# New places in the instruction order around the second and third routing of an attention and mixture-of-experts kernel

## The chip, the cores and the metric

The kernel runs on one core of one Trainium2 chip. The metric is the device time of one execution in microseconds. Three runs of the kernel before took 711.42, 707.03 and 711.97 us; their median is 711.42 us.

## The reference

First comes an attention over q, k, v of shape (8, 8, 576, 64). It is the sum of two: a full attention over sequences averaged in groups of four, its output repeated four times, and a local one, in which a position sees those less than four away. Its output, seen as 4608 tokens of 512 numbers, is the input of a layer with 8 experts. A gate gives each token a logit for each expert. All logits are gone through from the largest down, and a token goes to the expert of the logit if the token is still free and the expert has fewer than 576 tokens:

```
for idx in np.argsort(-flat):
    tok, e = idx // E, idx % E
    if assigned[tok] >= 0 or counts[e] >= cap: continue
    assigned[tok] = e; counts[e] += 1
out[mask] = np.maximum(x[mask] @ w1[e], 0) @ w2[e]     # mask: tokens of e
```

w1[e] is 512 by 1024, w2[e] is 1024 by 512.

## The kernel before

**Stages.** Attention takes the first 276 us. Then each expert has a routing, which finds the next expert that fills up and the list of its 576 tokens, a gather of these tokens, a split of its weights and an MLP. The routing for the next expert runs beside the MLP of the present one, so that eight MLPs stand one behind the other. Below, "the first MLP" is that of the first expert, and "the third routing" is the one that makes the third expert's list; it runs beside the second MLP, and it begins at the end of the first.

**Routing** (`phase`, L1007). A threshold is found in six rounds: three on the high 16 bits of the keys, three on the low ones. A round (`count`, L856) compares all keys with 64 or 32 thresholds (VectorE, L822; the first of each half is `first_compare`, L836, into a tile `level`), counts with 18 or 9 small matmuls (L871), takes differences and a flag (L881, L884), adds the flags up in one matmul (L889) and makes the next thresholds (L894 to L901). Between the halves stands a sum of the tokens above the threshold (`totals`, L917), behind the sixth round two matmuls that rank the chosen tokens (L928, L929), eighteen that make the list (L1131), and another sum. These matmuls make 17 groups, whose first ones are kept in `self.groups`. The list itself, `idx`, is four VectorE instructions (L1144); the last is `done`.

**Gather** (L1208). Five indirect DMAs of GpSimd (L1217) fetch 128, 128, 128, 128 and 64 tokens. For the first two experts TensorE turns each piece with four transposes (L1234), whose result ScalarE copies to fp16 (L1238) and whose rest VectorE makes (L1239, kept in `self.lows`: places 0 to 4 belong to the first expert, 5 to 9 to the second). Later experts turn their pieces by DMA (L1248). Pieces 0 and 1, and 2 and 3, share a PSUM tile of two banks.

**Weights** (`split`, L1190). Eight slices: ScalarE makes the fp16 high part (L1200), VectorE two halves of the low part (L1202). Slices 0 to 3 belong to w1, and are asked for behind the output of chunks 0 to 3 of the MLP in front.

**MLP** (L1262). Eight times twelve matmuls with 256 columns (pieces 0 and 1) and as many with 320 (pieces 2 to 4) make the hidden layer (L1279). Then five chunks of 24 matmuls with 512 columns (L1320) make the output; `second[c, j]` is matmul j of chunk c. A list `marks` has each matmul's place in the order, counted in microseconds of columns at 2.4 GHz; one MLP is 46.08 long on that scale.

**Order.** Each engine takes its instructions in a fixed order. A planner makes it from priorities and its own estimate of times; `behind_` (L832) and `issue_after` put an instruction behind another of its engine without a wait in the hardware. What matters here:

- `SPIN` (L1352): filler matmuls in front of the first MLP (L1186): 44, then the transposes of piece 0, 6 more, piece 1, 4 more, the MLP.
- `BEHIND` (L1344): the second routing's ranking behind `second[1, 6]`, its list behind `second[2, 2]` of the first MLP.
- `GET0` (L1343): the second expert's pieces 0 and 1 are asked for behind chunk 3 of the first MLP, 2 to 4 behind chunk 4.
- `PACE` and `PACES` (L1350): from the third routing on, a place for each of the 17 groups. A place less 19 is a mark in the MLP beside that routing; a negative one counts back from 47 in the MLP in front (`place`, L1253). A group isn't put in front of its place; how far behind it comes is the planner's choice. The third routing uses `PACE`, the fourth a table of its own.

Of the kernel before, what the change touches and what calls it, by code (L numbers as in the profile page):

```python
# [12 lines left out]
OP = mybir.AluOpType  # L13
# [722 lines left out]
LOP = 512  # L736
# [27 lines left out]
class Routing:  # L764
# [71 lines left out]
    def first_compare(self, i, key):  # L836
        cmp = self.compare(self.level[i], key, self.first, 0, NT)
        for ins in self.listed:
            self.behind_(cmp, ins)
        return self.level[i]  # L840

    def busy(self, n, mm):

# [163 lines left out]
    def phase(self, last, first=False, known=None):  # L1007

        nc, wk = self.nc, self.wk
        B3 = [128, E, NT]  # L1010

        def t(name, dt=BF, shape=(128, NT)):
            return wk.tile(list(shape), dt, name=name)
# [15 lines left out]
        if first:  # L1029
            self.pads = self.ps.tile([128, 2, 512], F32, name="pH", bufs=2)[:, 0, :E * NT]  # L1030
            xh = self.v["xh"]
            early = self.level[0]
# [5 lines left out]
        kh, kl = [self.v["s"].bitcast(I16)[:, o::2] for o in (1, 0)]  # L1038

        if not first:  # L1040
            early = self.first_compare(0, xh)
        if first:
            cmp0 = self.level[1]
            H = self.count(oh, xh, early, lambda: self.cap, None, lambda: self.compare(cmp0, xl, self.first, self.rest, NT))
        else:
            H = self.count(oh, xh, early, lambda: self.cap)
            cmp0 = self.first_compare(1, xl)
        e = t("e")
        nc.vector.tensor_scalar(e, kh, H, None, op0=OP.is_equal)
        ol = t("ol", BF, (128, E, NT))  # L1050
# [98 lines left out]
class Experts:  # L1149
# [40 lines left out]
    def split(self, raw, first):  # L1190

        nc = self.nc
        w = {}

        def piece(k):
            r = raw[k // 2][:, 1024 * (k % 2):1024 * (k % 2) + 1024]
            hi = self.wt.tile([128, 1024], F16, name=f"wh{k}")
            lo = self.wt.tile([128, 1024], F16, name=f"wl{k}")
            sc = W1S if k < 4 else W2S
            nc.scalar.activation(hi, r, AF.Copy, scale=sc)  # L1200
            for a in range(0, 1024, LOP):
                nc.vector.scalar_tensor_tensor(lo[:, a:a + LOP], r[:, a:a + LOP], sc, hi[:, a:a + LOP],  # L1202
                                               op0=OP.mult, op1=OP.subtract)
            w[k] = (hi, lo)

        return w, piece
# [133 lines left out]
TOP = 10 ** 6  # L1340
WS = {0: (4,), 1: (5,), 2: (6,), 3: (7,)}
GET = {0: (0, 1), 1: (2, 3), 2: (4,)}
GET0 = {3: (0, 1), 4: (2, 3, 4)}  # L1343
BEHIND = ((1, 6), (2, 2))  # L1344
TURN = (6, 12, 18)
NXT = 1
SPAN = 47.0
LAST = (2, 2.7, 10.4)
LEAD = -19.0
PACE = (0.6, 4, 10.5, 13, 15.3, 17, 18.5, 19.2, 21.5, 24, 26.5, 30, 32.5, 36.5, 37.2, 43.9, 43)  # L1350
PACES = {2: (0.6, 4, 10.5, 13.9, 16.2, 18, 19.5, 20.4, 22.5, 24.8, 27, 30, 32.5, 36.5, 37.2, 43.9, 43)}
SPIN = (44, 6, 4)  # L1352


def moe_attention(tc, q, k, v, wg, w1, w2, cst, out):
    nc = tc.nc
    with ExitStack() as top:
# [13 lines left out]
        with ExitStack() as ctx:  # L1371
# [21 lines left out]
            for i in range(E):  # L1393
                mine = split
                more = i + 1 < E
                if more:
                    with tc.high_priority(), tc.issue_after(ex.lows[NXT].ins if i == 0 else ro.done.ins) if i < 2 else nullcontext():
                        idx2, raw = ro.phase(i + 2 == E, False, lambda ei: ex.weights(ei, False))
                    w2_, split = ex.split(raw, False)
                    xt2, piece2 = ex.gather(idx2, False, i + 1 < ROWS)  # L1400
                    if i < FREE:
                        for k in range(8):
                            split(k)

                def in1(f, ins):
                    if f in WS:
                        with tc.issue_after(ins.ins), tc.high_priority(TOP if i == 0 else None):
                            for k in WS[f]:
                                mine(k)

                def in2(c, ins, mm):
                    if i == 0:
                        with tc.issue_after(mm.ins):
                            for j in GET0.get(c, ()):
                                piece2(j)
                    if more:
                        with tc.issue_after(ins.ins):
                            for j in GET.get(c, ()) if i else ():
                                piece2(j)
                            if c < 4:  # L1420
                                with tc.issue_after(ro.done.ins) if c and i == 0 else nullcontext():
                                    split(c)

                ex.mlp(w, xt, idx, in1, in2, i == 0)
                if i == 0:
                    ro.behind_(ex.products[0], ex.spins[2][-1])
                    for at, mms in zip(TURN, ex.turns[2:5]):
                        for mm in mms:
                            ro.behind_(mm, ex.products[at])
                    for at, mms in zip(BEHIND, ro.late):  # L1430
                        for mm in mms:
                            ro.behind_(mm, ex.second[at])
                elif more:
                    ex.place(i, ro.groups)
                ro.behind = ex.turned if i == 0 else None
                if more:
                    idx, w, xt = idx2, w2_, xt2
# [54 lines left out]
```

## Time and profile before

| | us |
|---|---|
| runs of the kernel before | 711.42, 707.03, 711.97 |
| median | 711.42 |
| the profiled execution's own time | 709.79 |
| its span, first to last instruction | 708.1 |
| attention | 0 to 276.0 of the span |
| rest of the first routing, filler and first transposes | 276.0 to 290.3 |
| eight MLPs | 290.3 to 697.5 |

The span is 1.7 us shorter than the profiled execution's time, which is 1.6 us below the median. TensorE is busy for 403.06 of the 407.20 us of the MLPs, VectorE for 290.85, ScalarE for 154.76. The granted clock is 1.00 there and 0.72 on average in the 14.3 us in front of them. Times of rows below are microseconds from the start of the span.

### The profile page before, as it was taken

What the parts mean: (1) busy time and instruction counts of PE and PEld (TensorE: products, weight loads), DVE (VectorE), ACT (ScalarE), POOL (GpSimd) and SP (SyncE); (2) the same over time, 40 slices, a digit from 0 to 9 for tenths busy, and PEclk for the clock granted to TensorE, in tenths of its full rate; (3) what the DMA queues carried; (4) which work ended last, traced back from release to release, by engine and by line L of the source; (5) the groups of instructions that cost most, each with busy time, mean ns of one, the idle gap of its engine ahead of it and who ended that gap; (6) DMA issues with size and microseconds to landing.
All of it is one profiled execution on the core that took longest, in us unless ns stands there. A gap on an engine that the chain in (4) does not pass through costs nothing.

```text
span 708.1 us, 21934 instructions
## 1 busy us (share of the span) xinstructions
PE 649.8 (92%) x8938; PEld 451.0 (64%) x8938; DVE 533.6 (75%) x1562; ACT 337.7 (48%) x650; POOL 232.7 (33%) x303
## 2 busy tenths in 40 slices
PE   6888999889999845999999999999999999999994
PEld 4667878778787733774574575575674674755741
DVE  5798889987989977887889697797797876634500
ACT  4567778787785521532532443443444424424410
POOL 4865374644737420402402303204104106202011
PEclk9899999999999975999999999999999999999997
DMA  9967859777785632605507617638348269814001
GB/s 263 245 157 218 227 159 245 205 205 202 197 238 160 192 117 89 218 1 181 192 1 283 157 43 269 129 116 229 95 183 204 55 233 198 313 35 100 1 31 38
DMA packets 132157, 113.73 MB, mean 161 GB/s; under 512 B 81240, under 2 KB 109912, under 8 KB 132056
## 3 DMA queue, kind: packets, MB, share of 16 engines
q1 hardware_dynamic: 124760, 90.76, 45.0%
q0 software_dynamic: 6432, 20.98, 9.5%
q8 instruction: 71, 1.16, 0.7%
q10 hardware_dynamic: 864, 0.58, 0.3%
q14 instruction: 30, 0.25, 0.1%
HBM read 85.74 MB, written 19.46 MB: 149 GB/s over the span
## 4 chain that ended last, share of the span: by engine, by line
PE 45%; DVE 22%; issue 17%; ACT 5%; DMA 5%; POOL 4%; SPq 1%; ACTq 0%; POOLq 0%; DVEq 0%
PE pH L1279 13%; PE pX L1320 11%; PE g L574 3%; PE pR L871 2%; DVE wl L1202 2%; PE g L327 2%; POOL out_dram L1330 2%; DVE x L453 2%; PE g L552 2%; PE g L592 2%; PE s L532 1%; DVE qt L311 1%; POOL xg L1217 1%; PE g L407 1%; PE pH L1186 1%
## 5 line engine op out<-in xcount | busy, mean ns | idle before, releaser
L1279 PE MATMUL pH<-xt,wh 128*128 128x256 f16 (+1 forms) x1024 | 191.3, 286 | 1.2 <-ACT xt L1238 0.5
L1320 PE MATMUL pX<-wh,ht 128*128 128x512 f16 (+1 forms) x640 | 178.0, 379 | 0.0
L1279 PE MATMUL pH<-xt,wl 128*128 128x320 f16 (+1 forms) x512 | 144.6, 286 | 0.0
L1320 PEld LDWEIGHTS <-ht 128*128 128x128 f16 (+1 forms) x960 | 82.6, 100 | 93.9 <-issue 3.8
L1320 PE MATMUL pX<-wl,ht 128*128 128x512 f16 (+1 forms) x320 | 117.6, 379 | 0.0
L1279 PEld LDWEIGHTS <-wh 128*128 128x128 f16 x1024 | 97.5, 98 | 30.2 <-issue 5.7
L1330 POOL DMA_INDIRECT out_dram<-y,idx x40 | 43.0, 1074 | 177.8 <-ACT y L1327 153.5
L1303 ACT ACTIVATE ht<-pH 128x512 f16<-128x512 f32 (+1 forms) x128 | 45.5, 407 | 112.5 <-PE pH L1279 112.5
L1202 DVE SCALAR_TENSOR_TENSOR wl<-nat,wh 128x512 f16<-128x512 f32 x128 | 83.5, 687 | 14.9 <-ACT wh L1200 8.3
L1327 ACT ACTIVATE y<-pX 128x512 f32<-128x512 f32 (+1 forms) x40 | 23.8, 594 | 103.4 <-PE pX L1320 54.3
L1306 DVE SCALAR_TENSOR_TENSOR ht<-pH,ht 128x512 f16<-128x512 f32 (+1 forms) x128 | 52.3, 450 | 24.4 <-ACT ht L1303 23.9
L1200 ACT ACTIVATE wh<-nat 128x1024 f16<-128x1024 f32 x64 | 67.3, 1053 | 4.1 <-DMA nat<-in_moe_w_dram 4.1
L1217 POOL DMA_INDIRECT xg<-x_dram,idx x40 | 42.5, 1062 | 61.9 <-DVE used L1100 33.4
L1279 PEld LDWEIGHTS <-wl 128*128 128x128 f16 x512 | 49.9, 98 | 12.7 <-issue 0.8
L563 ACT COPY pt<-g 64x512 f32<-64x512 f32 x72 | 41.8, 581 | 28.8 <-PE g L552 27.8
L574 PE MATMUL g<-vw,pt 128*64 128x65 f32 x1152 | 45.5, 229 | 5.6 <-issue 2.7
L574 PEld LDWEIGHTS g<-vw,pt 128*64 128x64 f32 x1152 | 39.6, 142 | 12.7 <-issue 6.6
L327 PE MATMUL g<-ident,nat 128*128 128x128 f32 x256 | 40.4, 283 | 3.9 <-DMA nat<-in_q_dram 3.3
L313 ACT COPY kt<-g 64x512 f32<-64x512 f32 (+1 forms) x60 | 38.3, 639 | 6.2 <-PE g L327 5.2
L1246 DVE SCALAR_TENSOR_TENSOR xs<-xg,xs 128x512 f16<-128x512 f32 (+1 forms) x30 | 20.3, 688 | 26.8 <-ACT xs L1245 15.7
L1019 POOL MEMSET f<- 128x1 bf16 x8 | 0.8, 106 | 116.3 <-DVE sumf L925 44.2
L300 POOL TENSOR_TENSOR gtmp<-kt 128x576 f32<-128x576 f32 x14 | 16.1, 1147 | 61.4 <-ACT kt L313 43.6
(221 smaller groups left out, 1153.0 us busy)
## 6 DMA issues: line engine op xcount, KB each, us to landing
nat<-in_moe_w_dram SPq DMA_DIRECT2D x28, 1024.0 KB
vw<-in_v_dram SPq DMA_DIRECT2D x136, 78.0 KB
x_dram<-x SPq DMA_DIRECT2D x36, 256.0 KB
nat<-in_q_dram SPq DMA_DIRECT2D x32, 256.0 KB
nat<-in_k_dram SPq DMA_DIRECT2D x32, 256.0 KB
nat<-in_v_dram SPq DMA_DIRECT2D x28, 256.0 KB
up<-up_dram SPq DMA_DIRECT2D x9, 256.0 KB
nat<-in_moe_w_dram SPq DMA_DIRECT2D x4, 512.0 KB
```

Source lines behind the costliest of these rows:

```text
L313: self.nc.scalar.copy(out, in_)
L327: nc.tensor.transpose(p[:, a, :, fp], src[:, 4 * hh + 2 * a + s, 2 * fp:2 * fp + 2].rearrange("p f d -> p (f d)"), self.ident)
L563: self.nc.scalar.copy(out, in_)
L574: nc.tensor.matmul(o[64 * i:64 * i + 64, 65 * h:65 * h + 65], pt[:, 2 * (h % 2) + i, 2 * g + h // 2].rearrange("p b q -> p (b q)"), self.v ...
L1200: nc.scalar.activation(hi, r, AF.Copy, scale=sc)
L1202: nc.vector.scalar_tensor_tensor(lo[:, a:a + LOP], r[:, a:a + LOP], sc, hi[:, a:a + LOP], op0=OP.mult, op1=OP.subtract)
L1217: self.fetched = nc.gpsimd.indirect_dma_start(out=xg[:n], out_offset=None, in_=self.x, in_offset=bass.IndirectOffsetOnAxis(ap=idx[:n, c:c ...
L1279: mm = nc.tensor.matmul(p[:, s, :s1 - s0], w[d][a][:, 128 * f:128 * f + 128], xt[:, b, d, s0:s1], start=j == 0, stop=j == len(seq) - 1)
L1303: last = nc.scalar.activation(hi, q, AF.Relu)
L1306: low = nc.vector.scalar_tensor_tensor(lo, q, 0.0, hi, op0=OP.max, op1=OP.subtract)
L1320: mm = nc.tensor.matmul(p[o:o + m], ht[:, f, h0:h0 + m], w[4 + f // 2][b][:, 512 * (f % 2):512 * (f % 2) + 512], start=j < parts, stop=j > ...
L1330: i = nc.gpsimd.indirect_dma_start(out=self.out, in_=y[:n], in_offset=None, out_offset=bass.IndirectOffsetOnAxis(ap=idx[:n, c:c + 1], axis=0))
```

## The change

- The first run of filler matmuls in front of the first MLP goes from 44 to 36.
- The second expert's list goes from behind `second[2, 2]` to behind `second[2, 0]`. Its piece 0 is asked for behind chunk 2 instead of chunk 3 of the first MLP, and piece 2 behind chunk 3 instead of chunk 4. Each piece's transposes get a place: behind `second[3, 20]`, `[4, 2]`, `[4, 8]`, `[4, 14]` and `[4, 20]`. The last two are still asked for behind the end of chunk 4.
- On VectorE, the low parts of the second expert's slice 0 go behind the finished list, those of slice 2 behind the rest of piece 0, and those of slice 3 behind the rest of piece 1. The third routing's first comparison of low bits goes behind the rest of piece 0 as well.
- The third routing gets a table of places of its own, the fourth's is replaced, and the fifth gets one.

Beside that, `first_compare` returns the instruction instead of the tile, and `split` keeps the low parts' instructions.

```diff
@@ first_compare
-        return self.level[i]
+        return cmp
@@ phase
         else:
             H = self.count(oh, xh, early, lambda: self.cap)
             cmp0 = self.first_compare(1, xl)
+            if self.behind:
+                self.behind_(cmp0, self.turned)
+            cmp0 = self.level[1]
@@ split
+                self.wlo.setdefault(k, []).append(nc.vector.scalar_tensor_tensor(
+                    lo[:, a:a + LOP], r[:, a:a + LOP], sc, hi[:, a:a + LOP], op0=OP.mult, op1=OP.subtract))
@@ constants
-GET0 = {3: (0, 1), 4: (2, 3, 4)}
-BEHIND = ((1, 6), (2, 2))
+GET0 = {2: (0,), 3: (1, 2), 4: (3, 4)}
+BEHIND = ((1, 6), (2, 0))
+TURN2 = ((3, 20), (4, 2), (4, 8), (4, 14), (4, 20))
-PACES = {2: (0.6, 4, 10.5, 13.9, 16.2, 18, 19.5, 20.4, 22.5, 24.8, 27, 30, 32.5, 36.5, 37.2, 43.9, 43)}
-SPIN = (44, 6, 4)
+PACES = {1: (18.1, 20.2, 21.3, 22.6, 24.6, 27.2, 29.3, 30, 31.9, 35, 36.8, 38.2, 40, 42.9, 43.8, 48.5, 50.5),
+         2: (6, 7.2, 13, 17, 18.8, 20.6, 22.2, 23, 24.6, 28, 30, 32, 34, 37.4, 38.2, 44.5, 44),
+         3: (2.5, 5, 11.5, 15.5, 17.2, 18.8, 20.2, 21, 22.6, 25, 27.5, 30.6, 33, 36.8, 37.6, 43.9, 43)}
+SPIN = (36, 6, 4)
@@ moe_attention, after the first MLP
-                    for at, mms in zip(BEHIND, ro.late):
+                    for at, mms in zip(BEHIND + TURN2, ro.late + ex.turns[5:]):
                         for mm in mms:
                             ro.behind_(mm, ex.second[at])
+                    for k, ins in ((0, ro.done), (2, ex.lows[5]), (3, ex.lows[6])):
+                        for low in ex.wlo[k]:
+                            ro.behind_(low, ins)
+                    ro.turned = ex.lows[5]
```

## Rows read from the trace of the kernel before

**Rows 1.** The page: busy time of each engine (share of the span) and instructions.

```profile
PE 649.8 (92%) x8938; PEld 451.0 (64%) x8938; DVE 533.6 (75%) x1562; ACT 337.7 (48%) x650; POOL 232.7 (33%) x303
```

**Rows 2.** Windows, first to fourth MLP: length, busy by engine, clock, DMA share, GB/s.

```profile
290.30:347.10 56.80, 55.47 (x459) 34.52 (x459) 48.82 (x148) 22.35 (x44) 13.14 (x13) 1.00 0.43 157
347.10:402.36 55.26, 53.12 (x442) 32.24 (x439) 46.40 (x149) 20.42 (x39) 10.98 (x11) 1.00 0.46 141
402.36:453.65 51.29, 50.74 (x415) 31.65 (x414) 41.86 (x132) 20.61 (x38) 10.51 (x11) 1.00 0.54 151
453.65:503.87 50.22, 50.16 (x415) 31.82 (x413) 41.52 (x130) 20.48 (x38) 10.26 (x11) 1.00 0.52 155
```

**Rows 3.** Chain of waits, in front of the first MLP: start, duration, what.

```profile
281.05 6.96 PE pH L1186 x44
...
288.44 0.73 PE pH L1186 x6
...
289.65 0.61 ACT xt L1238
```

**Rows 4.** Windows of TensorE alone, filler matmuls: length, busy, clock, DMA share, GB/s.

```profile
280.98:284.00 3.02, 3.02 (x15) 0.50 0.98 339
284.00:287.84 3.84, 3.84 (x33) 1.00 0.59 188
```

**Rows 5.** Timeline of GpSimd and ScalarE: start, duration, what [idle before <-releaser].

```profile
284.89 1.30 POOL L1217 DMA_INDIRECT xg<-x_dram,idx  x1 [0.30 <-DVE wl L1202]
386.03 1.34 POOL L1217 DMA_INDIRECT xg<-x_dram,idx  x1 [0.30 <-issue]
390.13 0.63 ACT L1245 ACTIVATE xs<-xg 128x512 f16<-128x512 f32 x1 [1.44 <-DMA xg<-x_dram,idx]
```

**Rows 6.** Timeline of VectorE and TensorE around the second expert's list.

```profile
330.02 0.49 DVE L1122 TENSOR_TENSOR r<-ohh,t 128x648 f16<-128x648 f16 x1
331.13 0.61 PE L1131 MATMUL pR<-r,ohl 128*128 128x36 f16 x18
332.84 0.69 DVE L1202 SCALAR_TENSOR_TENSOR wl<-nat,wh 128x512 f16<-128x512 f32 x1
333.45 0.68 DVE L1144 TENSOR_SCALAR idx<-sm 32x5 int32<-32x5 int16 x4
```

**Rows 7.** Timeline of TensorE, from the first MLP's end into the second.

```profile
341.33 0.60 PE L1234 MATMUL pH<-ident,xg 128*128 128x128 f32 x4
343.44 0.66 PE L1234 MATMUL pH<-ident,xg 128*128 128x128 f32 x4
348.08 0.60 PE L1234 MATMUL pH<-ident,xg 128*128 128x128 f32 x4
349.36 0.30 PE L1279 MATMUL pH<-xt,wh 128*128 128x320 f16 x1 [0.33 <-ACT xt L1238]
350.09 0.30 PE L1279 MATMUL pH<-xt,wh 128*128 128x320 f16 x1 [0.43 <-DVE xt L1239]
```

**Rows 8.** Timeline of VectorE, end of the first MLP.

```profile
339.87 1.35 DVE L822 TENSOR_TENSOR level<-xl,first 128x2304 bf16<-128x2304 int16 x1
342.69 0.69 DVE L1239 SCALAR_TENSOR_TENSOR xt<-pH,xt 128x512 f16<-128x512 f32 x1
```

**Rows 9.** Timeline of TensorE, matmuls of the third and fourth routing.

```profile
362.64 0.17 PE L889 MATMUL pR<-flag,one 128*128 128x8 bf16 x1
365.95 0.39 PE L871 MATMUL pR<-ol,cmp 128*128 128x32 bf16 x9
385.38 0.61 PE L871 MATMUL pR<-oh,level 128*128 128x16 bf16 x18 [0.51 <-DVE oh L993]
399.98 0.39 PE L871 MATMUL pR<-oh,cmp 128*128 128x32 bf16 x9
402.77 0.17 PE L889 MATMUL pR<-flag,one 128*128 128x8 bf16 x1
```

**Rows 10.** Waits of VectorE in the second MLP: in total, times, longest (us).

```profile
DVE nj L894 <- PE pR L889: 2.2, 6, 0.4
```

More of the change, by code (lines that the diff above doesn't have):

```diff
@@ L1040, in phase @@
         if not first:
-            early = self.first_compare(0, xh)
+            self.first_compare(0, xh)
+            early = self.level[0]
         if first:
@@ L1193, in split @@
         w = {}
+        self.wlo = {}
         def piece(k):
@@ L1201, in piece @@
             for a in range(0, 1024, LOP):
-                nc.vector.scalar_tensor_tensor(lo[:, a:a + LOP], r[:, a:a + LOP], sc, hi[:, a:a + LOP],
-                                               op0=OP.mult, op1=OP.subtract)
+                self.wlo.setdefault(k, []).append(nc.vector.scalar_tensor_tensor(
+                    lo[:, a:a + LOP], r[:, a:a + LOP], sc, hi[:, a:a + LOP], op0=OP.mult, op1=OP.subtract))
             w[k] = (hi, lo)
```

## The prediction, made before the change was run

> **What bounds the kernel now.** I read the page first: TensorE is busy for 92% of the span and VectorE for 75% [rows 1]. Then I cut the span at the MLPs [rows 2]. The fourth MLP takes 50.22 us with 0.06 us of idle TensorE; the first three take 56.80, 55.26 and 51.29, with 1.33, 2.14 and 0.55 idle. So TensorE sets the pace everywhere, and what can be won without less work lies in the first three, and in front of them, where the chain of waits runs through 44 filler matmuls for 6.96 us [rows 3]. The timelines then tell what the extra time is: transposes of the second expert, and matmuls of the routing that come up in TensorE's order before VectorE has made their operands [rows 7, 9].
>
> How far TensorE's idle time measures this has to be settled first. At 2.4 GHz 320 columns take 0.13 us, but such a matmul is shown as 0.30 [rows 7]: matmuls overlap in the record, so a wait of up to some 0.17 us shows no idle time. The lengths of the MLPs are thus the better measure. The Trainium skill (Perfetto Trace Analysis, "Identifying the Most-Contended Engine") says so too: busy time of matmuls is a poor measure, because they are pipelined. I sum by lengths below and name the sum by idle time beside it.
>
> **Fillers: 8 fewer.** The six later ones take 0.73 us, 0.12 each [rows 3]. The clock is at 2.4 GHz from 284.0 on, while the run is still going [rows 4], so those cut are fast ones: 8 x 0.12 = 0.97 us at most. What then comes next is piece 1 of the gather. Its issue starts at 284.89; a later gather, started at 386.03, was read at 390.13, 4.10 us on [rows 5]. With that latency piece 1 would be there at 288.99, while its transposes now start after the six fillers end at 289.17: a gain of 0.2. The data of this gather isn't seen landing; at 0.97 earlier its transposes would want it at 288.2, 3.3 us after the issue. Ends: 0 and -0.97. DMA queues are less full here (0.59 against 0.98 [rows 4]), so I take -0.6.
>
> **Second expert's list and transposes.** The list's matmuls go two matmuls of 512 columns (0.43 us) forward, to about 330.70; their operand r is finished at 330.51 [rows 6], so no new wait. On VectorE one low part of weights stood in front of the list and pushed it by 333.45 - 332.84 = 0.61 us [rows 6]; it now follows. GpSimd's five gathers begin 1.04 us earlier, and nothing else moves on its queue or on SyncE's.
>
> Piece 0's transposes go from 341.33 to four matmuls of 0.21 before chunk 3's end, about 340.5. The gather covers this with its 1.04; if the weights under way hold it back all the same, TensorE waits there for up to 0.85. Piece 1's transposes started at 343.44, 0.06 behind the end of piece 0's rest at 343.38 [rows 7, 8]: the two share a PSUM tile. That rest ended 1.5 us behind its transposes (341.33 + 0.53, four at full rate), and only four matmuls of chunk 3 and two half-width ones of chunk 4, 1.07 us, now stand between them: a new wait of about 0.4. In return, piece 3's transposes no longer stand inside the second MLP at 348.08, where the first matmuls of 320 columns waited for its copy (0.33 idle) and its rest (350.09 - 349.36 - 0.13 = 0.60) [rows 7]. The last two pieces stay behind chunk 4, since they are asked for there; but the place is at least 1 us earlier than 348.08, and the twelve matmuls of 256 columns cover copy and rest. So -0.9 + 0.4 = -0.5; ends -0.9 and +0.85.
>
> VectorE pays in order: four low parts (0.69 each) and one comparison of 1.35 [rows 6, 8] now wait for the rests of pieces 0 and 1, 4.1 us behind 342.5. Before the second MLP starts there are 4.8 us, with three rests of 0.69 to fit in as well: 1.4 too many. I cost this at nothing, because the comparison serves the second half of the routing, ten microseconds later; without that cover see the rival on VectorE.
>
> **Places of the third to fifth routing.** The second MLP is 5.04 us longer than the fourth [rows 2]. It holds one piece's transposes more (0.6) and some five routing groups more, two of nine matmuls (0.39) and three single ones (0.17) [rows 9], 1.3 if nothing overlapped and some 0.7 as it does. That leaves 3.7 of waiting, of which 0.9 is counted above: 2.8. The third MLP is 1.07 longer than the fourth, with the same groups. Together 3.9; by idle time, without the 0.76 at 349.36 and 350.09, it is 1.38 + 0.55 = 1.9.
>
> The new places put columns between a group and the next. Where they suffice, I see from the pairs: from 362.64 to 365.95 the chain took 3.31 us, and the new places 31.9 and 35 leave 3.1 + 0.17 = 3.27: covered. The fourth's pair from 399.98 to 402.77 took 2.79, and 18.8 to 20.6 leave 1.8 + 0.39 = 2.2: 0.6 stays. The first wait of the fourth, 0.51 at 385.38 [rows 9], goes, as its place is 2.9 us of columns later. I take two thirds of 3.9: -2.6; ends 0 and -3.9 (by idle time two thirds would be -1.3). Late next is the third expert's list, 2.4 us of columns later. It was also late in clock time by the waits in front of it, so its distance from the second MLP's start hardly changes; the end of that MLP comes nearer by about 3 us.
>
> **Sum.** -0.6 - 0.5 - 2.6 = -3.7 us. On the profiled execution's 709.79 this is 706.1, on the median, 1.63 higher, 707.7. The runs lie from 707.0 to 712.0, so the median of three is itself uncertain by more than this distance; I forecast the middle, 706.9.
>
> **Rivals.**
> - *The waits come back elsewhere.* VectorE works through the same list of instructions, and where its round trip is the limit, later places move the wait and don't remove it. For: VectorE is busy for 46.40 of the second MLP's 55.26 us [rows 2]. Against: the fourth MLP has 41.52 of 50.22 and no idle TensorE. Only the fillers' part is left: 709.8 - 0.6, with the median's offset 709.2 to 710.8.
> - *VectorE becomes the bound of the second MLP, slower than before.* Its idle time there, 8.9 us, is replies it has to wait for, such as 2.2 us in six waits for the flags' sum [rows 10]. If the five instructions held back, 4.1 us, all run past 347.1 and none of that idle time shrinks, the MLP takes 46.4 + 4.1 + 8.9 = 59.4: +4.1. With the fillers' gain 709.8 + 4.1 - 0.6 = 713.3 (714.9 on the median). It decides from the point where low parts of slice 3 end behind the first matmuls that use them, about 1 us into the second MLP. Against: by the count above the surplus is 1.4 us, and the comparison can take it.
> - *The clock.* Fillers ran 3.02 us at 1.2 GHz before 2.4 was granted [rows 4]. The change removes work from just behind that rise, and if TensorE then waits for the gather, the clock could fall again. As long a stretch at half rate costs 1.5 us: 706.9 + 0.6 + 1.5 = 709.0. Against: 36 fillers still reach past 284.0. The Trainium skill (TensorE: Matmul & The Clock Gate, Part 1) holds the slow clock to be the default, which activity lifts; the rise within the fillers agrees.
> - *The change doesn't do what it says*, in one part: places `[4, 14]` and `[4, 20]` can't take effect, as said. This is in the sum.
>
> **Chances.** Forecast 0.70; waits that come back 0.17; VectorE as the bound 0.09; the clock 0.04. A measurement of this kernel tells about 1%, 7.1 us, from no change. All gains at their ends give -0.97 - 0.9 - 3.9 = -5.8, or 704.0 from the profiled execution; 704.3 is 1% below the median, so faster by over 1% needs nearly everything, or a lucky set of runs: 0.13. Slower by over 1% is 718.5, which no case reaches without such a set: 0.04. The rest, 0.83, is within 1%. The range goes from 703.0 (704.0 with 1 us of scatter) to 711.5, which takes in the waits that come back; it leaves out VectorE as the bound.
>
> **What would show it.** Right: the second MLP takes 52 to 53 us instead of 55.26, the third about 50.7, piece 3's transposes stand in front of the second MLP, no idle time at its first matmuls of 320 columns, and the fillers' run is about 1 us shorter with the transposes of piece 1 starting 0.4 to 0.9 earlier. Wrong: idle TensorE in front of piece 1's transposes of over 0.5 us (gather), first matmuls of the second MLP waiting for low parts, matmuls of the third MLP waiting for turned pieces, or routing matmuls that still wait at their new places.

## The result: slower by 0.9%

The changed kernel takes **717.17 us** (median; 711.12 to 722.07) where the kernel before, on the same chip, takes 709.24 (706.58 to 716.14): a ratio of **1.0094**, 95% interval 1.0076 to 1.0113 (the ratio is not the quotient of the two medians, which lie 7.9 us or 1.12% apart). The forecast was 706.9, in a range up to 711.5. A second set of runs gave 717.25, ratio 1.0067 [1.0032, 1.0103]. The profiled execution of after took 713.27 us, span 711.6, so it is one of the quicker ones.

Windows of its first four MLPs, in the columns of [rows 2] (line numbers in rows of the changed code are up to five higher than in the kernel before):

```profile
289.18:347.23 58.05, 56.30 (x464) 35.15 (x464) 49.26 (x149) 22.91 (x45) 13.09 (x12) 1.00 0.41 151
347.23:402.30 55.07, 52.29 (x430) 31.56 (x426) 44.98 (x144) 20.05 (x38) 15.46 (x11) 1.00 0.46 136
402.30:454.48 52.18, 50.95 (x424) 31.79 (x422) 42.87 (x134) 20.36 (x38) 11.26 (x11) 1.00 0.52 154
454.48:507.42 52.94, 50.86 (x415) 31.60 (x414) 42.18 (x133) 20.37 (x38) 11.70 (x11) 1.00 0.51 147
```

Against [rows 2] that is +1.25, -0.19, +0.89 and +2.72: 4.67 us more, where 3.1 less was forecast for the middle two. The first MLP starts at 289.18 instead of 290.30, but the first routing's list matmuls started 1.53 earlier as well (278.42 against 279.95), so the way from list to MLP grew by 0.4 between these two profiles, with eight fillers fewer. The later four MLPs are as before. Where the four lose it, in the timeline of TensorE (idle time and what ended it in brackets):

```profile
279.18 4.58 PE L1190 MATMUL pH<-codes,one 128*128 128x288 bf16 x36
286.66 0.66 PE L1239 MATMUL pX<-ident,xg 128*128 128x128 f32 x4 [2.90 <-DMA xg<-x_dram,idx]
287.15 0.90 PE L1190 MATMUL pH<-codes,one 128*128 128x288 bf16 x6
287.89 0.60 PE L1239 MATMUL pX<-ident,xg 128*128 128x128 f32 x4
...
298.33 0.39 PE L1284 MATMUL pH<-xt,wh 128*128 128x256 f16 x2 [1.50 <-DVE ht L1311]
...
382.03 0.62 PE L1135 MATMUL pR<-r,ohl 128*128 128x36 f16 x18 [0.24 <-DVE ohl L1132]
...
400.99 0.17 PE L889 MATMUL pR<-flag,one 128*128 128x8 bf16 x1 [1.94 <-DVE flag L884]
...
485.53 0.18 PE L917 MATMUL pR<-sums,one 128*128 128x8 bf16 x1 [1.18 <-DVE sums L915]
```

All waits but the first name VectorE. Behind the 36 fillers TensorE waits for the gather of piece 0; piece 1's transposes, behind the next six fillers, wait for nothing. One wait stands early in the first MLP, one in front of the third list, one late in the second MLP (the fourth routing's flag), one in the fourth (the fifth routing's sums). What the transposes were moved for did happen. The same timeline, where [rows 7] have the pieces:

```profile
340.12 0.60 PE L1239 MATMUL pH<-ident,xg 128*128 128x128 f32 x4
...
342.29 0.66 PE L1239 MATMUL pH<-ident,xg 128*128 128x128 f32 x4
343.21 0.66 PE L1239 MATMUL pH<-ident,xg 128*128 128x128 f32 x4
...
345.84 0.66 PE L1239 MATMUL pH<-ident,xg 128*128 128x128 f32 x4
...
349.26 0.43 PE L1284 MATMUL pH<-xt,wh 128*128 128x320 f16 x2
```

All five pieces of the second expert are turned (transposed) before the second MLP starts at 347.23, and its first matmuls of 320 columns wait for nothing, where [rows 7] had 0.33 and 0.43.

The second execution of after that was profiled took 719.20 us, with a second MLP of 59.06 instead of 55.07. There ScalarE's and TensorE's timelines, and two windows of TensorE (length, busy, clock, DMA share, GB/s), are

```profile
397.21 0.63 ACT L1250 ACTIVATE xs<-xg 128x512 f16<-128x512 f32 x1 [2.00 <-DMA xg<-x_dram,idx]
401.14 0.63 ACT L1250 ACTIVATE xs<-xg 128x512 f16<-128x512 f32 x1 [3.31 <-DMA xg<-x_dram,idx]
401.68 0.58 ACT L1332 ACTIVATE y<-pX 128x512 f32<-128x512 f32 x1
```

```profile
402.31 0.38 PE L1325 MATMUL pX<-wh,ht 128*64 128x512 f16 x1 [2.87 <-ACT y L1332]
...
405.95 0.17 PE L889 MATMUL pR<-flag,one 128*128 128x8 bf16 x1 [1.33 <-DVE flag L884]
```

```profile
399.00:402.30 3.30, 0.43 (x3) 1.00 0.97 168
403.30:410.10 6.80, 5.47 (x30) 0.50 0.61 149
```

The eviction of the second layer's third chunk (y) stands on ScalarE behind four casts (xs, ScalarE's copies of the third expert's gathered pieces to fp16), each behind its gather; the fourth gather landed late, TensorE stood for 2.87 us, and then the clock was at 1.2 GHz for 6.8. The four MLPs of this execution sum to 222.18, 8.6 more than before, those of the first to 4.7 more; the median lies 7.9 above before's.

### The profile page after: what moved, and what is told of

It is laid out like the page before. It is cut to its first block, busy times and chain, and to the rows that moved or that the text cites. A ratio compares the mean times of both kernels' runs of the same rounds, so it can differ in the third digit from the quotient of the medians.

```text
span 711.6 us, 21914 instructions
## 1 busy us (share of the span) xinstructions
PE 647.5 (91%) x8930; PEld 448.6 (63%) x8930; DVE 535.2 (75%) x1562; ACT 337.6 (47%) x650; POOL 239.4 (34%) x303
## 4 chain that ended last, share of the span: by engine, by line
PE 41%; DVE 21%; issue 19%; DMA 7%; ACT 6%; POOL 4%; SPq 1%; POOLq 0%; ACTq 0%; DVEq 0%
PE pH L1284 11%; PE pX L1325 11%; PE g L574 2%; PE g L327 2%; DMA xg<-x_dram,idx 2%; POOL xg L1222 2%; POOL out_dram L1335 2%; PE g L552 2%; PE pR L871 2%; PE s L532 2%; DVE wl L1207 2%; PE g L592 1%; DVE x L453 1%; DVE ht L1311 1%; DVE qt L311 1%
## 5 line engine op out<-in xcount | busy, mean ns | idle before, releaser
L1335 POOL DMA_INDIRECT out_dram<-y,idx x40 | 46.4, 1161 | 171.9 <-ACT y L1332 146.5
L1332 ACT ACTIVATE y<-pX 128x512 f32<-128x512 f32 (+1 forms) x40 | 23.7, 594 | 103.7 <-PE pX L1325 51.2
L1311 DVE SCALAR_TENSOR_TENSOR ht<-pH,ht 128x512 f16<-128x512 f32 (+1 forms) x128 | 52.6, 451 | 23.5 <-ACT ht L1308 22.3
L1222 POOL DMA_INDIRECT xg<-x_dram,idx x40 | 45.6, 1139 | 57.5 <-DVE used L1104 21.8
L300 POOL TENSOR_TENSOR gtmp<-kt 128x576 f32<-128x576 f32 x14 | 16.0, 1146 | 60.3 <-ACT kt L313 43.4
```

The lines of the kernel that those rows point to most:

```text
L1222: self.fetched = nc.gpsimd.indirect_dma_start(out=xg[:n], out_offset=None, in_=self.x, in_offset=bass.IndirectOffsetOnAxis(ap=idx[:n, c:c ...
L1311: low = nc.vector.scalar_tensor_tensor(lo, q, 0.0, hi, op0=OP.max, op1=OP.subtract)
L1335: i = nc.gpsimd.indirect_dma_start(out=self.out, in_=y[:n], in_offset=None, out_offset=bass.IndirectOffsetOnAxis(ap=idx[:n, c:c + 1], axis=0))
```

## Experiments

Each kernel was timed beside the kernel before; ratios are to it. Lengths are of the first to fourth MLP in the one profiled execution. Some of them repeat closely: the first came out at 56.80 and 58.05 in before and after, and at 58.04 to 58.12 in five more profiles with after's order there. Others don't: the second took 55.07 and 59.06 in after's two profiles, and the third, 51.29 in before, took 50.69 in three other kernels with the same places for the fourth and fifth routing. So a difference of under 1 us between two single profiles isn't safe by itself. Where I give offsets into an MLP, they are starts of TensorE's or GpSimd's instructions less the MLP's start. Names in the diffs are shortened.

| kernel | ratio [95%] | first to fourth MLP, us |
|---|---|---|
| before | | 56.80, 55.26, 51.29, 50.22 |
| after | 1.0094 [1.0076, 1.0113] | 58.05, 55.07, 52.18, 52.94 |
| after once more | 1.0067 [1.0032, 1.0103] | 58.05, 59.06, 52.43, 52.64 |
| 36 fillers alone | 1.0014 [0.9987, 1.0041] | 57.36, 56.20, 50.69, 50.21 |
| list and transposes alone | 1.0005 [0.9978, 1.0032] | 57.19, 55.82, 50.69, 50.22 |
| three tables alone | 1.0045 [1.0025, 1.0065] | 56.50, 55.51, 52.51, 53.21 |
| after with 44 fillers | 1.0040 [1.0016, 1.0064] | 57.18, 54.34, 51.53, 53.93 |
| third's table alone | 1.0033 [1.0002, 1.0064] | 56.52, 57.01, 50.69, 50.22 |
| fourth's table alone | 1.0041 [1.0011, 1.0070] | 56.51, 55.96, 52.05, 50.24 |
| fifth's table alone | 1.0099 [1.0069, 1.0130] | 56.53, 55.74, 55.83, 52.62 |
| after, VectorE: compare ahead of rests | 1.0062 [1.0031, 1.0092] | 58.09, 54.70, 53.11, 52.64 |
| after, VectorE: sums ahead of compares | 1.0082 [1.0048, 1.0116] | 58.04, 58.14, 51.56, 51.61 |
| after, three orders | 1.0068 [1.0038, 1.0098] | 57.34, 57.91, 51.62, 51.29 |
| list and transposes, last rest behind | 1.0005 [0.9976, 1.0034] | 57.18, 54.50, 51.63, 51.19 |
| list and transposes, low parts not held | 1.0017 [0.9990, 1.0043] | 57.21, 56.56, 51.46, 50.22 |
| after, casts behind the eviction | 1.0093 [1.0058, 1.0128] | 58.12, 54.78, 53.81, 52.64 |
| after, low parts not held | 1.0089 [1.0054, 1.0124] | 58.07, 56.44, 52.18, 52.64 |
| after, all orders | 1.0047 [1.0022, 1.0073] | 57.34, 52.86, 54.32, 51.69 |
| list and transposes, orders mended | 1.0005 [0.9976, 1.0033] | 57.19, 54.09, 52.04, 50.22 |

**One part at a time.** Four kernels: the fillers, the list with the transposes, the tables, and all but the fillers.

```diff
-SPIN = (44, 6, 4)
+SPIN = (36, 6, 4)
```

> The kernel before with 36 fillers instead of 44 and nothing else. Theory A (fillers and clock: fewer fillers let the clock fall or rise late in part of the executions, and this is a good part of the 0.94%): 0.3 to 0.6% slower than before, with a lower mean clock. Theory B (the loss is in VectorE's order and in the new places, from the first MLP to the fourth): 0.0 to 0.2% faster, the first MLP starting about 1 us earlier. Since the planner works with its own times, the order of VectorE in the first MLP may change; then B expects the wait of 1.50 us for a hidden layer's low part, seen at 298.33 in the changed kernel, here as well, and no gain.

Neither faster nor, by the interval, slower. TensorE waits 2.47 us for piece 0's gather, and 1.49 at 300.28 in the first MLP for its hidden layer's low part, as after does at 298.33.

```diff
-PACES = {1: (18.1, ...), 2: (6, 7.2, ...), 3: (2.5, 5, ...)}
-SPIN = (36, 6, 4)
+PACES = {2: (0.6, 4, 10.5, ...)}
+SPIN = (44, 6, 4)
```

> The second expert's list, transposes and VectorE's order as changed; 44 fillers and the places of before. Theory B1 (the new places are what costs): within 0.2% of before, first MLP plus second MLP together no longer than 112 us. Theory B2 (VectorE's order around the second expert's list costs, and what follows is only its echo): 0.5 to 0.9% slower. Theory A: same as before.

No change of time. The waits of [rows 7] are gone here too, and 1.30 us idle has come up at 401.49, for the fourth routing's compare.

```diff
-PACES = {2: (0.6, 4, 10.5, ...)}
+PACES = {1: (18.1, ...), 2: (6, 7.2, ...), 3: (2.5, 5, ...)}
```

> The kernel before with the new tables of places for the third to fifth routing and nothing else. Theory B1: 0.4 to 0.8% slower, with the third and fourth MLP together at about 105 us instead of 101.5, and waits of over 1 us for a flag or a sum in the second to fourth MLP. Theory B2: within 0.2% of before. Theory A: same as before or up to 0.4% faster, as forecast.

Slower by 0.45%, some 3.2 us: third MLP +1.22, fourth +2.99. The places, which were to bring 2.6 us, cost about that by themselves.

```diff
-SPIN = (36, 6, 4)
+SPIN = (44, 6, 4)
```

> The changed kernel with 44 fillers again. Theory A: most of the loss goes, within 0.4% of before. Theory B: 0.7 to 1.0% slower than before still, with the waits of the changed kernel in the third and fourth MLP.

0.5% less than after's first ratio, but the intervals of this run and of after's second overlap: what the fillers add to after isn't told apart from 0. The three parts alone give 0.14, 0.05 and 0.45%, together 0.64%, where after gave 0.94 and 0.67.

**One table at a time**, on the kernel before.

```diff
+         1: (18.1, 20.2, 21.3, ..., 42.9, 43.8, 48.5, 50.5),
```

> The kernel before with the new table of places for the third routing alone. Theory C (the third expert's list comes later, so its gather lands later, and VectorE, which takes its instructions in order, waits for the gathered pieces with the fourth routing's comparisons and flags behind them): second and third MLP together 0.5 to 1.5 us longer than the 106.55 us of before, an idle TensorE of over 0.5 us in front of a flag or a comparison of the fourth routing late in the second MLP, the fourth MLP still at 50.2. Theory D (the places of the third routing are right, and those of the fourth and fifth cost): second and third MLP together 105.0 to 106.5.

Second and third MLP together take 107.70 instead of 106.55, as theory C has it. In TensorE's timeline there is

```profile
399.39 0.39 PE L871 MATMUL pR<-oh,cmp 128*128 128x32 bf16 x9 [2.10 <-DVE cmp L822]
```

With its new places the third list's matmuls come 35.1 us into the second MLP, where before has them at 32.7, and the third expert's first gather is issued at 39.9 instead of 37.6.

```diff
-         2: (0.6, 4, 10.5, 13.9, ...)
+         2: (6, 7.2, 13, 17, ...)
```

> The kernel before with the new table for the fourth routing alone. Theory C: third MLP within 0.5 us of the 51.29 of before, fourth MLP at 50.2. Theory D: third MLP 1 to 1.5 us longer than before, and, as the fourth expert's list is hardly later, the fourth MLP at 50.2 to 50.7.

Third MLP +0.76 (+1.36 against the 50.69 of three other kernels), second +0.70 (the flag waits 1.93 us at 392.46), fourth as before: nearer to theory D.

```diff
+         3: (2.5, 5, 11.5, 15.5, ...)
```

> The kernel before with a table of its own for the fifth routing and nothing else. With all three new tables the fourth MLP took 53.21 us instead of 50.22. Theory D1 (the fifth's own places do this: they put VectorE's sum behind the next routing's comparisons and a flag behind low parts of weights): third MLP as before, fourth MLP 52.5 to 53.5. Theory D2 (it is an echo of the later fourth routing): fourth MLP at 50.2 to 50.6.

The worst of the three: fourth MLP +2.40, as theory D1 has it, and third +4.54, which neither theory had. TensorE's timeline, and windows of TensorE before and after that instruction:

```profile
441.34 0.18 PE L889 MATMUL pR<-flag,one 128*128 128x8 bf16 x1 [3.31 <-DVE flag L884]
```

```profile
438.00:441.30 3.30, 0.02 (x1) 1.00 0.83 195
442.20:445.60 3.40, 3.40 (x9) 0.50 0.99 248
```

After's two profiles don't have this wait of 3.31 us. What they share is the fourth MLP: with the fifth's table and the order that the planner makes of it, it takes 52.6 to 53.9 in every profile; without the table 50.2 to 51.2. The one-table ratios sum to 1.73%, the three tables together cost 0.45%: a table's cost alone, such as the wait of 3.31 us, can't be carried over into after.

**After once more.**

> The changed kernel once more, on the same chip as the three. MLP lengths as in its first profile (58.0, 55.1, 52.2, 52.9, within 0.3 us each) if they are set by the order of instructions; time 0.7 to 1.0% above before. If the loss beyond the 4.7 us of the MLPs is in the clock in front of the first MLP, its mean clock is lower than that of before in these runs too.

717.25 us: the loss is there again. Its profile is shown above: the first, third and fourth MLP repeat within 0.3 us, the second does not. The mean granted clock was lower too, 0.9647 over after's six runs against 0.9681 over the 26 of before beside them.

**Orders on VectorE and ScalarE.** From here on instructions only change places on one engine.

```diff
+ro.behind_(third_rests[0], fourth.compare_2)
```

> The changed kernel with one thing moved on VectorE alone: in the second MLP the fourth routing's second-level threshold and compare stand ahead of the third expert's first two rests (xs, each behind its gather), TensorE's order is the same. Theory C (TensorE's idle time late in the second MLP comes from VectorE's order: a threshold 0.2 us long stands behind a rest that waits for a gather): compare done at about 390.7 instead of 394.6, the flag's 1.94 us wait of TensorE at 400.99 falls under 0.5, second MLP 53.1 to 53.9 instead of 55.07, and fewer executions with the clock falling there, 2 to 4 us off the median against the changed kernel (713 to 715). Rival (the wait is set by the gathers or by the list's lateness itself): the wait stays above 1.3 us, second MLP within 0.4 of 55.1, median 716 to 718.

The theory fails in this form. The compare was done 4 us earlier, the flag still kept TensorE waiting for 1.79 us, for the flag itself stood behind the later rests. The second MLP took 54.70, the third lost 0.93 more, and the median, 717.02, is after's.

```diff
+self.listed += [self.summed]   # next routing's compares stand behind the sums, from the second routing on
```

> The changed kernel with one thing moved in the fourth MLP: VectorE's sums of the fifth routing stand ahead of the sixth routing's two level compares. Theory D1 (the fourth MLP is longer by TensorE's waits at the fifth routing's new places, the largest of them VectorE's own order): the 1.18 us wait on the sums is gone, fourth MLP 51.6 to 52.0 instead of 52.94, median 0.5 to 1.2 us below the changed kernel's. Rival D2 (only the place among the MLP's matmuls counts, whatever VectorE's order): fourth MLP 52.7 to 53.1.

The first theory holds: the 1.18 us wait is gone and the fourth MLP takes 51.61. In after VectorE's order had been

```profile
481.47 1.36 DVE L822 TENSOR_TENSOR level<-xh,first 128x2304 bf16<-128x2304 int16 x1
...
483.47 1.36 DVE L822 TENSOR_TENSOR level<-xl,first 128x2304 bf16<-128x2304 int16 x1
...
485.04 0.43 DVE L915 TENSOR_REDUCE sums<-og 128x8 bf16<-128x288 bf16 x1
```

with the sums' operand ready at 474.28. In the median, 716.6, nothing shows that is clear of the noise: this profile has the 2.94 us wait for y and 1.93 for the flag.

```diff
+ro.behind_(second.compare_0, first_mlp.low[1])
```

> The changed kernel with both orders above and a third: the second routing's level compare stands behind the low parts of the first MLP's second hidden tile. Theory A2 (the 36 fillers start the first MLP 1.1 us earlier, and TensorE gives it back at 298.33 because VectorE's 1.35 us compare stands ahead of the low part it waits for): the 1.50 us wait falls under 0.4 and the first MLP goes from 58.05 to 56.8 to 57.2; with the two others the four MLPs sum to 214.5 to 216 instead of 218.2, median 711 to 714. If the three orders explain all of the loss, the sum is 213.6 or less and the median is within 1 us of the kernel before's. Rival (each order only moves a wait): sum 217 to 218.5, median 715 to 718.

The compare goes behind the second low part that the first MLP makes, which is still its first hidden tile's. The 1.50 us wait fell to 0.67, not under 0.4, and 0.7 us of its 1.25 came back; the fourth took 51.29. The second had waits of 3.02 for y and 1.93 for the flag. So the sum is 218.16, as the rival has it, by the second MLP alone.

```diff
+ro.behind_(third_rests[4], fourth.compare_3)   # on list and transposes alone
```

> The second list and transposes alone (44 fillers, the places of before), with the third expert's last rest behind the fourth routing's third-level compare on VectorE. In the run without that order TensorE waited 1.30 us for that compare at 401.49. Theory C: that wait falls under 0.4, second MLP 54.3 to 54.8 instead of 55.82, median 0.3 to 1.5 us below the kernel before's (ratio 0.998 to 0.9995). Rival: the last rest is needed early in the third MLP and the same 1 us is lost there (third MLP 51.5 instead of 50.7), ratio 0.9995 to 1.0015.

The second MLP went from 55.82 to 54.50 as expected, and 0.94 came back in the third, as the rival had it, and 0.97 in the fourth, whose flag waited 0.69 us at 498.65. No gain.

```diff
-for k, ins in ((0, ro.done), (2, ex.lows[5]), (3, ex.lows[6])):
+for k, ins in ():
```

> The second list and transposes alone (44 fillers, the places of before), without the holds on VectorE: low parts of the second expert's slices 2 and 3 may stand in front of the rests of pieces 0 and 1. Theory H (what VectorE holds back delays the third routing: its first flag reaches TensorE 2.6 us into the second MLP instead of 1.6, its list 34.8 instead of 32.7, and the gathers of the third expert that follow later give the gain back late in the MLP): first flag at 1.6 to 2.0, list at 32.5 to 33.5, waits behind 395 us under 0.6 each, second MLP 53.6 to 54.6 instead of 55.82, ratio 0.996 to 0.9995. Rival H2 (without the holds the rests come late and TensorE waits for them): 0.3 to 0.6 us more idle before the first matmuls of 320 columns, second MLP 55.3 or more, ratio 1.000 to 1.002.

> The changed kernel without the holds on VectorE (low parts of the second expert's slices 0, 2 and 3). Theory H: as in the run without the other parts, first flag of the third routing at 1.6 to 2.0 us of the second MLP and its list before 34.0 instead of 34.8, late waits of the second MLP under 1 us, second MLP 53.5 to 54.5 and fewer falls of the clock, median 713 to 715. Rival (with the third table the places set the third routing, not the holds): list at 34.5 to 35.2, as where the table stood alone, second MLP 55 or more, median 716 to 718.

The holds are the orders that put low parts of weights behind the list and the rests. They are taken off once in the kernel with list and transposes alone, once in after; the third routing's comparison of low bits stays behind piece 0's rest in both. The third routing's first flag comes 1.7 us into the MLP instead of 2.6: the held-back low part had delayed it. The list comes at 34.0 and 34.2 instead of 34.8, so these holds are under half of its 2.1 us of lateness, and the wait late in the MLP stays (2.23 at 400.15, and 2.51). They cause a part of the lateness, and taking them off wins nothing.

```diff
+ro.behind_(third_casts[2], second_mlp.y[2])              # ScalarE
+ro.behind_(third_rests[0], fourth.compare_2)             # VectorE
+for x in third_rests[3:5]: ro.behind_(x, fourth.flag_2)  # VectorE
```

> The changed kernel, with three orders changed for the late second MLP: on ScalarE the third expert's third cast stands behind the eviction of the second layer's third chunk (in the changed kernel that eviction stands behind four casts, each behind its gather); on VectorE the fourth routing's second-level compare stands ahead of the third expert's rests, and its flag ahead of the last two. TensorE's order is the same. Theory C2 (both engines that stand between TensorE and its next operands wait in order for gathers): neither a wait for y of 2.9 us (seen in three of five executions of such kernels) nor one for the flag of 1.3 to 1.9 us, together under 0.6; second MLP 52.8 to 53.6, median 2 to 4 us below the changed kernel's (713 to 715). Rival (the gathers' lateness itself is what TensorE meets, at the next place): the fifth turned piece comes 1.5 to 3 us late in the third MLP, second and third MLP together 106.5 to 108, median 716 to 718.

The wait for y is gone, that for the flag isn't, and second and third MLP together take 108.59, more than in after's first profile (107.25). In VectorE's and TensorE's timelines:

```profile
401.94 0.69 DVE L1207 SCALAR_TENSOR_TENSOR wl<-nat,wh 128x512 f16<-128x512 f32 x1 [3.43 <-ACT wh L1205]
...
403.97 0.15 DVE L884 TENSOR_TENSOR flag<-pR,less 32x8 bf16<-32x8 f32 x1
```

```profile
404.18 0.17 PE L889 MATMUL pR<-flag,one 128*128 128x8 bf16 x1 [1.87 <-DVE flag L884]
...
407.56 0.39 PE L871 MATMUL pR<-oh,cmp 128*128 128x32 bf16 x9 [1.04 <-DVE cmp L822]
...
409.31 0.43 PE L1284 MATMUL pH<-xt,wh 128*128 128x320 f16 x2 [0.92 <-DMA xt<-xs]
```

A low part of weights stands in front of the flag and waits 3.43 us for ScalarE's copy, which stands behind the casts, which wait for the gathers: two queues long.

```diff
+for x in third.low_parts[2]: ro.behind_(x, fourth.flag_2)
...   # with the orders of the three runs above
```

> The changed kernel with every order that the runs so far have named: the orders of the run with the casts behind the eviction, and with them the third expert's low parts of slice 2 behind the fourth routing's second flag (in that run one of them stood ahead of the flag and waited 3.43 us for ScalarE's copy, which stood behind the casts); the fifth routing's sums ahead of the sixth's compares; the second routing's compare behind the first MLP's second low part. Places, fillers and TensorE's order are those of the changed kernel but for the first MLP. Theory C3 (in-order waiting behind the gathers on ScalarE and VectorE is what makes TensorE wait late in the second MLP): the wait for the flag falls from 1.87 us to under 0.4, second MLP 52.3 to 53.4, first 57.3, fourth 51.3 to 51.7, sum of four 212.5 to 215.5, median 711 to 714. Rival (late gathers are met at the next place): turned pieces come over 1.5 us late in the third MLP, its length 53.5 or more, sum of four 216 to 218.5, median 715 to 718.

The flag's wait is gone and the second MLP takes 52.86: in this one profile the in-order queues behind the gathers were the cause of the waits late in it. The ratio's interval lies below that of after's first, though it overlaps that of the second. But the third MLP takes 54.32: against after's first profile the second MLP won 2.21 and the third gave 2.14 back, against its second 6.20 and 1.89. So against the first profile 2 us are won in the first and fourth MLP and nothing in the other two; the sum of the four, 216.21, lies in the rival's range. TensorE's timeline in the third:

```profile
402.71 0.39 PE L871 MATMUL pR<-oh,cmp 128*128 128x32 bf16 x9 [1.20 <-DVE cmp L822]
...
404.74 0.43 PE L1284 MATMUL pH<-xt,wh 128*128 128x320 f16 x2 [1.19 <-DMA xt<-xs]
```

The gathers are as late as in after (issued 39.1 to 45.6 us into the second MLP), so a turned piece (xt) comes late as well: the order decides where TensorE meets them.

> The second list and transposes alone (44 fillers, the places of before) with the same orders for the late second MLP. Theory C3: no wait over 0.5 us after 385 us in the second MLP, its length 53.6 to 54.6 instead of 55.82, third 50.7 to 51.7, median 0 to 1.5 us below the kernel before's (ratio 0.998 to 1.000). Rival: turned pieces late in the third MLP by over 1 us, second and third together 106.3 or more, ratio 1.000 to 1.002.

Nearly the same orders for the late second MLP (the last rest and the low parts stand behind the comparison that follows the second flag) on list and transposes alone, without the tables: second MLP 54.09, third 52.04, with one wait of 1.10 in the third. Second and third together take 106.13, 0.42 less than before. The time doesn't change. No version tried beats the kernel before.

## Why the prediction was wrong

**Fillers, -0.6: nothing in front of the first MLP, and a wait in it.** The step priced the gather of piece 1 alone. What stands right behind the first run of fillers is piece 0, and its gather had no term. In before the 44 fillers cover it:

```profile
280.98 7.02 PE L1186 MATMUL pH<-codes,one 128*128 128x288 bf16 x44
287.84 0.60 PE L1234 MATMUL pX<-ident,xg 128*128 128x128 f32 x4
```

They reach to 4.80 us behind this gather's issue at 283.04. In after's chain of waits it takes

```profile
281.24 5.38 DMA xg<-x_dram,idx
286.62 0.04 issue
286.66 0.67 PE pX L1239 x4
```

and TensorE is idle for 2.90 us. The eight fillers cut are 0.97 of that. Another part is the clock: in before 15 fillers ran at 1.2 GHz [rows 4], in after's profile none, as the clock rose at 278.0, before the first of them. TensorE's windows there (length, busy, clock, DMA share, GB/s):

```profile
276.00:278.00 2.00, 2.00 (x9) 0.50 0.48 131
278.00:289.00 11.00, 7.77 (x73) 1.00 0.81 263
```

The 0.4 us by which the way from list to first MLP grew is no measure of the fillers: over all profiles that way took 9.67 to 11.49 us with 36 fillers (nine profiles, mean 10.4) and 9.83 to 11.20 with 44 (ten, mean 10.5). What the eight fillers do cost stands in the first MLP: 57.36 us with the fillers alone, 56.50 to 56.80 in the five kernels with 44 fillers and the list and transposes of before. With 36 fillers a matmul waits 1.48 to 1.51 us for a low part in seven profiles of nine (0.67 and 0.66 in the two with the comparison pushed back), with 44 in none. VectorE's timeline in before, then in after:

```profile
292.05 0.68 DVE L960 TENSOR_REDUCE m<-lm 128x36 f32<-128x288 f32 x1
...
296.39 1.35 DVE L822 TENSOR_TENSOR level<-xh,first 128x2304 bf16<-128x2304 int16 x1
```

```profile
293.79 0.65 DVE L960 TENSOR_REDUCE m<-lm 128x36 f32<-128x288 f32 x1
...
296.19 1.35 DVE L822 TENSOR_TENSOR level<-xh,first 128x2304 bf16<-128x2304 int16 x1
```

Counted from the first MLP's start, the maximum m comes at 1.75 us in before and at 4.62 in after, and the comparison at 6.09 and 7.01; the kernel with the fillers alone has 4.62 and 7.01 as well. The planner put m behind three rests of the first expert's pieces, and the low part stands behind the comparison. An order of VectorE that changes with the fillers had no term in the sum.

**List and transposes, -0.5: the waits went as forecast, the sum about 0.** The vanished waits of [rows 7] and the pieces in front of the second MLP came as forecast; the new wait of 0.4 us in front of piece 1 did not come. The step that failed is what VectorE holds back: "I cost this at nothing". The third routing's first flag came 1.0 us later into the second MLP, and its list 2.1 us later, at 34.8 instead of 32.7. The list's matmuls in before, then with list and transposes alone:

```profile
379.82 0.61 PE L1131 MATMUL pR<-r,ohl 128*128 128x36 f16 x18
```

```profile
382.85 0.62 PE L1135 MATMUL pR<-r,ohl 128*128 128x36 f16 x18 [0.24 <-DVE ohl L1132]
```

The list waits for only 0.24 us there: it stands later in TensorE's own order. The MLP's matmuls in front of it add up to 29.9 us of columns instead of 27.1. With the low parts not held the first flag is back at 1.7, but the list is still at 34.0, behind 29.2 us of columns. How much of the rest comes from the comparison that stayed held, and how much from the planner alone, no run tells.

**Places, -2.6: the step that decided the sign.** It took two thirds of 3.9 us of waiting as won; the tables alone cost 0.45%, some 3.2 us, instead. Two of its premises failed. It said that the third list's distance from the second MLP's start "hardly changes"; with the third's table alone it grew by 2.4 us, as much as the columns that the step itself names. (In after it grew by 2.1, but those aren't the table's: up to its list the third routing stands there within 0.02 us where list and transposes alone have it.) And it priced waits in the second and third MLP, but not the fifth's table, most of whose groups stand in a fourth MLP with 0.06 us of idle time [rows 2]: there was nothing to gain. It cost 2.4 there alone and 2.72 in after. 1.18 of that is one place on VectorE, where the sums fell behind two comparisons; what the planner makes of a later place on VectorE had no term in the sum. Put on top of list and transposes, the tables change the four MLPs by -0.01, -1.48, +0.84 and +3.71 us (after with 44 fillers against list and transposes alone): some waiting in the second MLP was won, and the fourth lost more.

**What the late list triggers** had no term either. The third expert's gathers go out later (in after's profile 39.1 to 45.8 us into the MLP, before 37.6 to 43.4), so ScalarE's casts and VectorE's rests wait for them in order, and an eviction, a flag and a compare that TensorE needs stand behind. This gave 1.94 us in one profile of after, and 4.2 us and a fall of the clock in the other. With the orders mended the waits are gone there in the profile with all orders, but some 2 us return in the third MLP.

**Rivals.** "The waits come back elsewhere" was the nearest: they did, and larger, since a waiting instruction in an in-order queue holds up others than its own reader. "VectorE as the bound" did not happen: it is busy for 44.98 of the second MLP's 55.07 us. The clock did not fall in front of the first MLP, where its rival looked for it, in spite of 2.90 us idle; it fell in the second MLP of the other profile. The 4.7 us of the first profile are accounted for by MLP. The way from there to the medians' distance of 7.9 (7.5 in the second set) stays open in part: in the second set after's mean clock was 0.0034 lower, which, as an estimate, is about 5 us more per run at 1.2 GHz, worth about 2.4. Where in the runs these lie, and how often the slower second MLP comes, two profiled executions don't tell.

## What to carry to other kernels

A later place for one engine's instruction is not a local change: a planner reorders the other queues around it, and whatever it puts behind a consumer of a DMA inherits the DMA's latency. Even eight fillers less on TensorE changed VectorE's order here. And price a wait at the first reader: behind the fillers that was piece 0, not piece 1. So follow each moved step to the DMAs that it issues, and list what stands behind their first consumers on every in-order engine. Give no new place to work in a stage that has no waits: the fourth MLP had 0.06 us to win and lost 2.4 and more.

## What was not expected of the hardware

TensorE's clock fell behind idle time in the middle of the MLPs: after 2.87 us of it to 1.2 GHz for 6.8 us, after 3.31 us for 3.4 us, and in after with the low parts not held after 2.51 us for 3.4. Idle stretches of 2.94 and 3.02 us in two other kernels, at the same place of the second MLP, were followed by none, nor was the one of 2.90 us in front of after's first MLP. What decides isn't shown here.

GpSimd's issue of a scatter, beside three of VectorE's comparisons in a row (380.63 to 384.52), lasted over four times as long as the same one in before, which starts behind them (0.98 us at 382.43):

```profile
381.02 4.34 POOL L1335 DMA_INDIRECT out_dram<-y,idx  x1 [2.71 <-ACT y L1332]
386.31 1.46 POOL L1222 DMA_INDIRECT xg<-x_dram,idx  x1 [0.95 <-DVE cap L1103]
```

It ends 0.84 us after the last comparison. The Trainium skill (SBUF — State Buffer, "Who interferes with whom") says that a VectorE instruction with two SBUF inputs contends with a GpSimd instruction that reads SBUF, but infers that the making of DMA descriptors escapes it when VectorE works on two tensors; this row speaks against the second half. No run tested it by itself. It cost nothing here, as the list was finished later, at 386.04.
